# Four of eight weight-chunk turns moved from TensorE to DMA transposes on ScalarE's queue

## The chip, the cores and the metric

The kernel runs on one core of a Trainium2 chip. The metric is device time in microseconds (us) for one launch, the median over runs. The engines are named as in the profile: PE is TensorE's matmul stream and PEld its weight loads, DVE is VectorE, ACT is ScalarE, POOL is GpSimd, and SP is SyncE, which issues most DMAs. ACT can issue DMAs too, from its own instruction stream.

## The reference

Linear attention is followed by a multiplicative feed-forward network, all of it without a softmax or an activation function:

```python
kv  = einsum('bhsd,bhse->bhde', k, v)                 # 8 batches, 8 heads, 576 tokens, 64 wide
out = einsum('bhsd,bhde->bhse', q, kv)
rms = sqrt(mean(out * out, axis=-1, keepdims=True) + 1e-06)
x   = out / rms * g_norm                              # then (4608 tokens, 512)
a, b = x @ w1, x @ w2                                 # 512 -> 1024
h   = a * b @ w3                                      # 1024 -> 1024
y   = h @ w_out                                       # 1024 -> 512
```

Everything is float32 inside the kernel. The four weight arrays reach the kernel as 64-bit words and are converted there.

## The kernel before

**The fold.** Since nothing stands between w3 and w_out, the kernel first multiplies the two into one matrix w3o (1024 x 512), held in `w3o_sb`. This takes place at the start, in two halves of 512 rows each. Each half goes over eight chunks of 128 columns of w3 (`c` = 0 to 7). For a chunk, a 128x512 piece of w3 has to be turned, four blocks of 128x128, before it can be the stationary operand of four matmuls (`fold_chunk`, L694) whose sums stay in four PSUM banks over all chunks.

**The turn.** `turn_w3(half, c)` does it on PE: four transposes (L681) into a PSUM bank with the tag "at", then an ACT copy (L686) of 128x512 into a place in the tile `ab`. There are four such places, one for each `c % 4`, and three "at" banks, which the turns share with query turns (L355), kv sums (L335), and products of attention (L413). The turn of chunk c+1 stands ahead of the last matmul of chunk c.

**What else is in the fold's second half.** The order on every engine is the order in which this loop is written; nothing rearranges it. Around the second half's chunks stand parts of attention for batch 0:
- `begin_q` (ahead of c = 1 and c = 4): eight PE transposes of queries in two "at" banks and two ACT copies `qT` (L357). `begin_kv`: 72 small matmuls (L335) into two "at" banks and six small ACT copies of the sums.
- `product` (behind c = 2 and c = 5): 64 small matmuls (L413), then the norm in steps: two squares on ACT (L380), two reduces on DVE (L381), the root on ACT (L385), the reciprocal (L387) and two multiplies (L390) on DVE, which write `xn`.
- `x_first`: the result of the first product is turned by DMA: `turn_by_dma` copies the 32-bit words apart into two planes of 16-bit words (a split, L294 or L296), issues a 16-bit DMA transpose on SP (L298), and puts the planes together again (a merge, L308).
- the conversion of the remaining raw weights in units of 128x1024 words. A unit has two ACT passes (L158, L160; `begin_next`) and four DVE operations (L162, L166, L169, L172; `end_next`); a unit of w1 and w2 is also scaled by `g_norm` on DVE (L135). The second half's units are numbered here by their place in the list `todo`: 8, 9, 11 and 13 hold the w3 chunks 0 and 1, 2 and 3, 4 and 5, 6 and 7 of the second half, and 10 and 12 are w1 and w2 units. One unit is ended, and the next begun, around each chunk.
- loads on SP: raw weights (L198), queries (L94), k and v (L104).

After the fold the kernel computes the feed-forward network by groups of 512 tokens, with fewer products by sums and differences of blocks (`winograd`, L724, L1016, L1274), and prepares the next batches of attention beside it. The w1 and w2 matmuls of the first group (L724) begin at 83.21 us.

The loop of the second half, as it was:

Of the kernel before, what the change touches and what calls it, by code (L numbers as in the profile page):

```python
# [22 lines left out]
def kernel(  # L23
# [32 lines left out]
    nc = tc.nc  # L56
    PSUM = bass.MemoryType.PSUM
    P = 128
# [5 lines left out]
    KF = DF // P  # L64
# [19 lines left out]
    def bank(pool, tag):  # L84
        return pool.tile([P, 512], FP32, name=tag, tag=tag)
# [6 lines left out]
    def load_q(b, r):  # L92
        t = loaded["q", b, r] = inp.tile([P, 2, J * D], FP32, name="q_sb")
        nc.sync.dma_start(  # L94
            out=t, in_=q[b, 2 * r:2 * r + 2, 0:G, :].rearrange("h (p j) d -> p h (j d)", j=J)
        )
# [20 lines left out]
    ab = [ab_all[:, i] for i in range(2)]  # L117
# [73 lines left out]
    def load_next():  # L191
        if len(raws) == len(todo):
            return
        what, i = todo[len(raws)]
        raw = raw_tile()

        def load(where, src):
            nc.sync.dma_start(out=raw[:, where].rearrange("p (c m) -> p c m", c=src.shape[1]), in_=src)  # L198

        if what == "w":  # L200
            for n, w in enumerate((w1, w2)):
                src = w[:, i * P:(i + 1) * P].rearrange("(c p) f -> p c f", p=P)
                load(slice(n * 512, (n + 1) * 512), src)
        elif what == "b":
            for h in range(2):
                src = w3[DF // 2:DF, (2 * i + h) * P:(2 * i + h + 1) * P]
                load(slice(h * 512, (h + 1) * 512), src.rearrange("(m p) f -> p m f", p=P))
        else:
            src = w3[0:DF // 2, i * P:(i + 1) * P].rearrange("(m p) f -> p m f", p=P)
            cols = w_out[i * P:(i + 1) * P, :].rearrange("p (c f) -> p c f", c=1)  # L210

            n = 1 if i else 2
            for h in range(n):
                load(slice(h * 512 // n, (h + 1) * 512 // n), src[:, h * NH // n:(h + 1) * NH // n, :])
            for h in range(n):
                f = slice(h * DM // n, (h + 1) * DM // n)
                load(slice(512 + f.start, 512 + f.stop), cols[:, :, f])
        raws.append(raw)

    converted = []  # L220
# [14 lines left out]
    begun = []  # L235
    in_first_group = False

    def begin_next(between=None):
        if len(begun) < len(todo):
            begun.append(conversions(len(begun)))  # L240
            for c in begun[-1]:
                next(c)
                if between is not None:
                    between()
                next(c)

    def end_next(load=True):
        for c in begun[len(converted)]:
            all_of(c)
        converted.append(len(converted))  # L250
        if load:
            load_next()

    def all_of(steps):
        for _ in steps:
            pass
# [14 lines left out]
    def keep_warm(n):  # L271

        t = bank(ps_mm, "mm")
        for _ in range(n):
            nc.tensor.matmul(t[:, 0:P], lhsT=ident, rhs=ident, start=True, stop=True)

    def turn_by_dma(srcs, apart, turned, dsts, copy=nc.gpsimd.tensor_copy):

        def words(t):
            return t.bitcast(U16).rearrange("p ... (n w) -> p ... n w", w=2)

        def planes(t, i, n):
            t = t.bitcast(U16).rearrange("p (w n) -> p w n", w=2)
            size = 4 * P // n
            return t[:, :, i * size:(i + 1) * size]

        for i, src in enumerate(srcs):  # L290
            to = planes(apart, i, len(srcs))
            if len(src.shape) == 3:
                src, to = words(src), to.rearrange("p w (a n) -> p w a n", a=src.shape[1])
                copy(to, src.rearrange("p a n w -> p w a n"))  # L294
            else:
                copy(to, words(src).rearrange("p n w -> p w n"))  # L296
        yield
        nc.sync.dma_start_transpose(  # L298
            out=turned.bitcast(U16).rearrange("p (a t) -> p a t", t=P), in_=apart.bitcast(U16)
        )  # L300
        yield
        for i, dst in enumerate(dsts):
            src = planes(turned, i, len(dsts))
            if len(dst.shape) == 3:
                src = src.rearrange("p w (a n) -> p a n w", a=dst.shape[1])
            else:
                src = src.rearrange("p w n -> p n w")
            copy(words(dst), src)  # L308
# [365 lines left out]

    w3T = {}

    def turn_w3(half, c):
        t_ps = bank(ps_at, "at").rearrange("p (m f) -> p m f", m=NH)
        for m in range(NH):
            src = chunks[:, c, 0, m * P:(m + 1) * P]  # L680
            nc.tensor.transpose(t_ps[:, m, :], src, ident)  # L681

        w3T[half, c] = ab[c % 4 // 2][:, c % 2].rearrange(
            "p i (a f) -> p (i a) f", f=P
        )
        nc.scalar.copy(w3T[half, c], t_ps)  # L686

    sums_ps = {}

# [700 lines left out]
    chunks = fold.tile([P, KF, 2, DM], FP32, name="chunks")  # L1390
    with tc.manual_schedule(
        engines={mybir.EngineType.DVE, mybir.EngineType.Activation, mybir.EngineType.SP}
    ):
        for _ in range(RAW):
            load_next()
        nc.scalar.activation(const.tile([P, 1], FP32, name="warm"), eps_col, AF.Sqrt)
        g_row = const.tile([1, P], FP32, name="g_row")
        for e in range(2):
            nc.scalar.dma_start(
                out=g_row[:, e * D:(e + 1) * D], in_=g_norm.rearrange("(o d) -> o d", o=1)  # L1400
            )


        keep_warm(14)
        begin_next()
        end_next()
        turn_w3(0, 0)
        keep_warm(9)
        begin_next()

        g_ps = bank(ps_at, "at")[:, 0:1]
        nc.tensor.transpose(g_ps, g_row, ident[0:1, 0:1])
        nc.scalar.copy(g_col, g_ps)
        for c in range(KF):

            if c:
                begin_next()
            end_next()
            if c == 4:
                load_four("k", 0, 0)  # L1420
                load_q(0, 0)
            elif c == 5:
                load_four("v", 0, 0)
                load_q(0, 1)
                load_q_left(0)
            fold_chunk(0, c, range(NH - 1))
            if c == 0:
                begin_next(lambda: turn_w3(0, 1))
            else:
                turn_w3(*((0, c + 1) if c + 1 < KF else (1, 0)))  # L1430
            fold_chunk(0, c, [NH - 1])
            if c == 0:
                keep_warm(2)


        first = batch(0)
        first.start()
        BEGIN, PRODUCT = {1: 0, 4: 1}, {2: 0, 5: 1}
        norms = {}
        FIRST = len(converted) + KF - 1  # L1440
        for c in range(KF):
            if c in BEGIN:
                first.begin_q(2 * BEGIN[c], 2 * BEGIN[c] + 1)
                if c == max(BEGIN):
                    x_first = first.x_by_dma(0, nc.scalar.copy)
                    next(x_first)
                    next(x_first)
            if c - 1 in norms:
                all_of(norms[c - 1])
            if c < KF - 2:  # L1450
                if c < max(BEGIN):
                    begin_next()
                if c == max(BEGIN) + 1:
                    all_of(x_first)

                end_next(len(raws) < FIRST)
            elif c == KF - 2:
                run(sum_w(0))
            fold_chunk(1, c, [0])
            if c in BEGIN:  # L1460
                first.begin_kv(BEGIN[c])
                if c == max(BEGIN):
                    load_q_left(1)
            if c + 1 == KF:
                for r in range(2):
                    first.turn(2 + r)
                run(combine_x(0))
                end_next(False)
                for _ in range(3):
                    load_next()  # L1470
            fold_chunk(1, c, range(1, NH - 1))
            if c + 1 < KF:
                turn_w3(1, c + 1)
            if c in (max(BEGIN), KF - 2):
                begin_next()
            fold_chunk(1, c, [NH - 1])
            if c in PRODUCT:
                norms[c] = first.product(PRODUCT[c])
                next(norms[c])
                next(norms[c])  # L1480
    fold_cm.__exit__(None, None, None)
    late_pool = ctx.enter_context(tc.tile_pool(name="late", bufs=1, reuse_waits="tile"))
# [6 lines left out]
    for n, T in enumerate(groups):  # L1489
# [29 lines left out]
        if T in IN_TWO:  # L1519
            p = 2  # L1520
# [130 lines left out]
```

## Time and profile before

| | |
|---|---|
| median of 3 runs | 744.86 us (744.6 to 745.33) |
| the profiled execution's own time | 745.0 us |
| its span, first to last instruction | 743.1 us |
| PE busy | 736.6 us (99%) |
| DVE, ACT busy | 629.4 us (85%), 378.7 us (51%) |
| granted TensorE clock | 1.000 |
| fold's second half and the attention in it, on PE | 46.66 to 83.21 us from its second turn on |

The profiled execution's time is 1.9 us longer than its span. A line of the chain of waits gives a start, a length and the work that the end of the program rests on at that time; a line of a timeline gives a start, the time from the first to the last of a run of equal instructions, and in brackets how long the engine had been idle and whom it waited for. L12 is line 12 of the kernel.

### The profile page before, as it was taken

The page shows a single profiled execution, that of the slowest core. Times are in us where ns is not written, and L with a number is a line of the kernel's source. Part 1 is how long each engine was busy: PE and PEld are TensorE (multiplying, and loading weights), DVE is VectorE, ACT ScalarE, POOL GpSimd, SP SyncE. Part 2 cuts the span into 40 slices and gives each one's busy share as a digit, 9 for nine tenths or more (in the row PEclk, how much of TensorE's full clock was granted, in tenths as well). Part 3 has the DMA queues.
Part 4 walks back from the last instruction along what each step waited for, and adds up shares of the span by engine and source line. Part 5 has one row for each costly group of instructions (what it writes and reads, how often), then busy time and mean ns, then how long its engine had stood idle before and what let it go on. Part 6 is the DMA issues. An engine that isn't in the chain of part 4 may idle for free.

```text
span 743.1 us, 16816 instructions
## 1 busy us (share of the span) xinstructions
PE 736.6 (99%) x6843; PEld 659.5 (89%) x6843; DVE 629.4 (85%) x1233; ACT 378.7 (51%) x652; POOL 21.8 (3%) x29
## 2 busy tenths in 40 slices
PE   8999999999999999999999999999999999999998
PEld 6455788888899999999999999999999999999997
DVE  6987998967869689978996899689969987997797
ACT  6687778424552575257526752576277313212321
POOL 0000000132000000010000001000001000000000
PEclk9999999999999999999999999999999999999999
DMA  9996934599999698869886988588848662565454
GB/s 307 366 321 208 263 108 122 122 331 307 281 307 321 176 264 271 267 159 284 258 265 158 304 255 263 184 279 241 278 101 220 220 212 87 176 215 162 135 198 135
DMA packets 135456, 169.65 MB, mean 228 GB/s; under 512 B 78036, under 2 KB 110804, under 8 KB 135380
## 3 DMA queue, kind: packets, MB, share of 16 engines
q1 hardware_dynamic: 132928, 154.16, 69.6%
q10 hardware_dynamic: 2452, 14.42, 5.7%
q8 instruction: 54, 0.88, 0.5%
q14 instruction: 22, 0.18, 0.1%
HBM read 130.55 MB, written 20.71 MB: 204 GB/s over the span
## 4 chain that ended last, share of the span: by engine, by line
PE 96%; DVE 1%; ACT 1%; DMA 1%; issue 0%; SPq 0%; ACTq 0%
PE mm L724 37%; PE mm L1274 23%; PE mm L1016 21%; PE mm L694 7%; PE at L335 2%; PE at L724 2%; PE at L413 1%; PE mm L413 1%; PE at L681 1%; DMA raw<-in_moe_w_out_dram 1%; PE at L1317 0%; DVE ab L162 0%; PE at L432 0%; ACT w_sb L133 0%; DVE chunks L169 0%
## 5 line engine op out<-in xcount | busy, mean ns | idle before, releaser
L1065 ACT COPY slots<-mm 128x512 f32<-128x512 f32 x88 | 51.7, 587 | 125.7 <-PE mm L1274 83.1
L724 PE MATMUL mm<-xT,w_sb 128*128 128x256 f32 x448 | 102.9, 379 | 0.0
L724 PEld LDWEIGHTS mm<-xT,w_sb 128*128 128x128 f32 x448 | 84.4, 190 | 11.5 <-issue 0.5
L724 PE MATMUL mm<-xc,ws 128*128 128x256 f32 x336 | 76.1, 379 | 0.0
L724 PEld LDWEIGHTS mm<-xc,ws 128*128 128x128 f32 x336 | 63.8, 190 | 8.7
L742 ACT COPY slots<-mm 128x512 f32<-128x512 f32 x59 | 34.6, 587 | 70.9 <-PE mm L724 65.5
L694 PE MATMUL mm<-chunks,ab 128*128 128x512 f32 x128 | 60.7, 605 | 0.7 <-DVE chunks L172 0.7
L1069 DVE TENSOR_TENSOR slots<-mm,slots 128x512 f32<-128x512 f32 x66 | 45.1, 683 | 17.3 <-PE mm L1016 17.3
L1066 ACT COPY slots<-mm 128x384 f32<-128x384 f32 x88 | 42.4, 482 | 25.8 <-PE mm L1274 23.1
L1016 PE MATMUL mm<-ws,w3o_sb 128*128 128x128 f32 x350 | 53.9, 275 | 0.0
L381 DVE TENSOR_REDUCE inv<-sq 128x8 f32<-128x512 f32 (+1 forms) x40 | 24.6, 629 | 29.9 <-ACT sq L380 29.9
L1274 PE MATMUL mm<-w3o_sb,ab 128*128 128x128 f32 x368 | 49.0, 276 | 0.0
L1016 PEld LDWEIGHTS mm<-ws,w3o_sb 128*128 128x128 f32 x350 | 46.4, 192 | 0.0
L1274 PEld LDWEIGHTS mm<-w3o_sb,ab 128*128 128x128 f32 x368 | 45.4, 192 | 0.6
L1274 PE MATMUL mm<-w3o_sb,raw 128*128 128x128 f32 x340 | 43.5, 275 | 0.0
L694 PEld LDWEIGHTS mm<-chunks,ab 128*128 128x128 f32 x128 | 21.6, 190 | 22.4 <-issue 14.4
L1274 PEld LDWEIGHTS mm<-w3o_sb,raw 128*128 128x128 f32 x340 | 40.7, 192 | 0.0
L724 PE MATMUL mm<-xc,w_sb 128*128 128x256 f32 x160 | 38.6, 384 | 0.3 <-ACT slots L742 0.3
L724 PE MATMUL mm<-xT,ws 128*128 128x256 f32 x160 | 38.1, 381 | 0.0
L1070 DVE TENSOR_TENSOR slots<-mm,slots 128x384 f32<-128x384 f32 x66 | 36.4, 551 | 1.9 <-PE mm L1274 1.9
L308 ACT COPY xT<-xn 128x1024 uint16<-128x1024 uint16 x28 | 32.5, 1168 | 3.3 <-DMA xn<-xT 3.3
L724 PEld LDWEIGHTS mm<-xc,w_sb 128*128 128x128 f32 x160 | 29.7, 190 | 4.9 <-ACT slots L742 0.7
(243 smaller groups left out, 1650.8 us busy)
## 6 DMA issues: line engine op xcount, KB each, us to landing
w3o_sb<-w_l SPq DMA_DIRECT2D x21, 896.0 KB, 4.9
w3o_sb<-w3o_l SPq DMA_DIRECT2D x18, 896.0 KB, 6.8
raw<-in_moe_w_dram SPq DMA_DIRECT2D x31, 512.0 KB, 7.4
raw<-w3o_l SPq DMA_DIRECT2D x15, 896.0 KB, 4.9
w3o_sb<-w3o_l ACTq DMA_DIRECT2D x14, 896.0 KB, 4.6
k_sb<-in_k_dram SPq DMA_DIRECT2D x16, 576.0 KB, 5.1
v_sb<-in_v_dram SPq DMA_DIRECT2D x16, 576.0 KB, 6.3
q_sb<-in_q_dram SPq DMA_DIRECT2D x32, 256.0 KB, 4.3
```

The source lines that it names most:

```text
L308: copy(words(dst), src)
L335: nc.tensor.matmul(ps[r * D:(r + 1) * D, :], lhsT=k_sb[rows, r, cols], rhs=v_sb[rows, r, cols], start=(j == 0), stop=(j == JS - 1),)
L381: adds["norm"] = nc.vector.tensor_reduce(out=inv[:, i], in_=sq.rearrange("p (h d) -> p h d", d=D), axis=AX.X, op=ALU.add)
L694: nc.tensor.matmul(sums_ps[half][m], lhsT=w3T[half, c][:, m, :], rhs=chunks[:, c, 1, :], start=(c == 0), stop=(c == KF - 1),)
L724: nc.tensor.matmul(ps[:, u, :], lhsT=lhsT(a_name, u, c), rhs=rhs(b_name, c),  start=(u == 0 and c == 0 and new), stop=(c == chunks - 1), s ...
L742: copies.setdefault(name, []).append(nc.scalar.copy(t, ps))
L1016: nc.tensor.matmul(ps[place // 4][:, place % 4, :], lhsT=x, rhs=y, start=new and place // 4 not in seen, stop=True, skip_group_check=True,)
L1065: nc.scalar.copy(z[:, 0:4], ps[0])
L1066: return nc.scalar.copy(z[:, 4:7], ps[1][:, 0:3])
L1069: nc.vector.tensor_add(z[:, 0:4], ps[0], z[:, 0:4])
L1070: nc.vector.tensor_add(z[:, 4:7], ps[1][:, 0:3], z[:, 4:7])
L1274: nc.tensor.matmul(ps[place // 4][:, place % 4, :], lhsT=x[:, c, :], rhs=y[:, c, :], start=new and place // 4 not in seen, stop=(c == 1), ...
```

## The change

In the fold's second half the chunks 2, 3, 4 and 5 are no longer turned on PE. VectorE splits the natural 128x512 piece into two planes of 16-bit words in its place in `ab`, a DMA transpose issued on ScalarE's queue turns the planes and writes them over the natural piece, and an ACT copy merges them into the place in `ab`. The chunks 0, 1, 6 and 7, and the whole first half, stay on PE.

The places of the steps in the loop are: splits and issues for 2 and 3 at c = 0, behind the end of unit 9; their merges at c = 1, behind the end of unit 10; splits of 4 and 5 at c = 2, behind the end of unit 11, and their issues behind the middle matmuls of c = 2; the merge of 4 between the squares and the root of the first norm; the merge of 5 at c = 3, where the turn for chunk 4 was. At c = 2 the four DVE operations of unit 12 are also issued, ahead of the first norm's; the scale by `g_norm` stays where it was, behind that norm.

```diff
-    def turn_by_dma(srcs, apart, turned, dsts, copy=nc.gpsimd.tensor_copy):
+    def turn_by_dma(
+        srcs, apart, turned, dsts, copy=nc.gpsimd.tensor_copy, split=None, queue=nc.sync
+    ):
...
-                copy(to, words(src).rearrange("p n w -> p w n"))
+                (split or copy)(to, words(src).rearrange("p n w -> p w n"))
         yield
-        nc.sync.dma_start_transpose(
+        queue.dma_start_transpose(
             out=turned.bitcast(U16).rearrange("p (a t) -> p a t", t=P), in_=apart.bitcast(U16)
         )
...
+    def w3_by_dma(c):
+        natural, to = chunks[:, c, 0, :], place_w3(1, c).rearrange("p m f -> p (m f)")
+        return turn_by_dma(
+            [natural], to, natural, [to], nc.scalar.copy, split=nc.vector.tensor_copy,
+            queue=nc.scalar,
         )
...
                 end_next(len(raws) < FIRST)
+                if c == 0:
+                    split_w3(2, 3)
+                    send_w3(2, 3)
+                elif c == 1:
+                    all_of(turns[2])
+                    all_of(turns[3])
+                elif c == 2:
+                    split_w3(4, 5)
+                    for steps_of_w in begun[len(converted)]:
+                        next(steps_of_w)
...
             fold_chunk(1, c, range(1, NH - 1))
-            if c + 1 < KF:
+            if c == 2:
+                send_w3(4, 5)
+            elif c == 3:
+                all_of(turns[5])
+            if c + 1 < KF and c + 1 not in turns:
                 turn_w3(1, c + 1)
...
                 norms[c] = first.product(PRODUCT[c])
                 next(norms[c])
+                if c == 2:
+                    all_of(turns[4])
                 next(norms[c])
```

`split_w3` runs the first step of `w3_by_dma` for each of its chunks, `send_w3` the second, and `all_of` the rest.

More of the change, by code (lines that the diff above doesn't have):

```diff
@@ L293, in turn_by_dma @@
                 src, to = words(src), to.rearrange("p w (a n) -> p w a n", a=src.shape[1])
-                copy(to, src.rearrange("p a n w -> p w a n"))
+                (split or copy)(to, src.rearrange("p a n w -> p w a n"))
             else:
-                copy(to, words(src).rearrange("p n w -> p w n"))
+                (split or copy)(to, words(src).rearrange("p n w -> p w n"))
         yield
-        nc.sync.dma_start_transpose(
+        queue.dma_start_transpose(
             out=turned.bitcast(U16).rearrange("p (a t) -> p a t", t=P), in_=apart.bitcast(U16)
@@ L675, with place_w3 @@
     w3T = {}
+    def place_w3(half, c):
+        w3T[half, c] = ab[c % 4 // 2][:, c % 2].rearrange("p i (a f) -> p (i a) f", f=P)
+        return w3T[half, c]
     def turn_w3(half, c):
@@ L681, in turn_w3 @@
             nc.tensor.transpose(t_ps[:, m, :], src, ident)
-        w3T[half, c] = ab[c % 4 // 2][:, c % 2].rearrange(
-            "p i (a f) -> p (i a) f", f=P
+        nc.scalar.copy(place_w3(half, c), t_ps)
+    def w3_by_dma(c):
[3 more added lines that the diff above has]
+            queue=nc.scalar,
         )
-        nc.scalar.copy(w3T[half, c], t_ps)
     sums_ps = {}
@@ L1440, with split_w3, send_w3 @@
         FIRST = len(converted) + KF - 1
+        turns = {}
+        def split_w3(*cs):
+            for c in cs:
+                turns[c] = w3_by_dma(c)
+                next(turns[c])
+        def send_w3(*cs):
+            for c in cs:
+                next(turns[c])
         for c in range(KF):
```

## The prediction

> **What bounds the kernel now.** I read the page first (shares by engine, then the chain that ended last), then the chain of waits between 44 and 84 us, then the timelines of ScalarE and VectorE there, then the DMA share by window and the DMA transposes' own rows.
>
> ```profile
> PE 736.6 (99%) x6843; PEld 659.5 (89%) x6843; DVE 629.4 (85%) x1233; ACT 378.7 (51%) x652; POOL 21.8 (3%) x29
> ...
> PE 96%; DVE 1%; ACT 1%; DMA 1%; issue 0%; SPq 0%; ACTq 0%
> ```
>
> TensorE (PE) is never idle for long: what leaves PE's stream may leave the time, if nothing else then comes last. ACT's 51% is an average over the whole span, so I look at the stage itself. The chain between 44 and 84 us is all PE:
>
> ```profile
> 46.66 0.44 PE at L681 x4
> 47.09 0.86 PE mm L694 x2
> 47.95 0.87 PE at L355 x8
> 48.83 0.86 PE mm L694 x2
> ...
> 52.81 0.44 PE at L681 x4
> ...
> 56.82 0.44 PE at L681 x4
> ...
> 58.12 1.09 PE at L413 x64
> ...
> 61.98 0.44 PE at L681 x4
> ...
> 63.28 0.87 PE at L355 x8
> ...
> 65.28 1.21 PE at L335 x72
> ...
> 68.40 0.44 PE at L681 x4
> ```
>
> Columns: start, length, what. The L681 pieces are the chunk turns; those at 52.81, 56.82, 61.98 and 68.40 (chunks 2 to 5) go. The second query turn (63.28) and the second kv product (65.28) stay. ScalarE beside them:
>
> ```profile
> 57.35 0.59 ACT L686 COPY ab<-at 128x512 f32<-128x512 f32 x1 [1.33 <-PE at L681]
> 59.26 1.09 ACT L380 ACTIVATE sq<-at 128x512 f32<-128x512 f32 x2 [1.32 <-PE at L413]
> 61.20 0.31 ACT L385 ACTIVATE inv<-inv,eps_col 128x16 f32<-128x16 f32 x1 [0.86 <-DVE inv L381]
> 61.42 1.17 ACT L158 ACTIVATE ab<-raw 128x1024 f32<-128x1024 uint32 x1
> 62.47 1.16 ACT L160 ACTIVATE chunks<-raw 128x1024 f32<-128x1024 f32 x1
> 63.51 0.60 ACT L686 COPY ab<-at 128x512 f32<-128x512 f32 x1
> 63.97 1.09 ACT L357 COPY qT<-at 128x512 f32<-128x512 f32 x2
> ```
>
> ACT waits for PE (brackets) up to the norm, and from the square root at 61.20 on it runs without a gap until 66.96. The first query copy ends at 63.97 + 0.60 = 64.57, only 0.71 before kv starts on PE at 65.28, and kv's second bank waits for that copy.
>
> **PE.** Removed: 16 transposes, 4 x 0.44 = 1.76 us. Nothing is added to PE. 1.76 is 0.24% of 744.86; about 0.2% (1.49 us) is what a measurement of this kernel can tell from no change, so nearly all of it must survive to count as faster.
>
> **Splits on VectorE.** Four copies of 128x1024 16-bit words. No row shows one on DVE. Bounds: 0.69 (TENSOR_SCALAR 128x1024, one source) and 1.23 (two-source 128x1024, L162); ScalarE's own split of that shape (L294) took 1.08. I take 0.69, since the form is one-source, SBUF to SBUF, and keep 1.23 for the range. The first two follow unit 9's last operation (ends 44.73) and delay unit 10 from 45.62 to 46.1; the 0.38 us that DVE idled before unit 11 (50.60) takes most of that up, so unit 11 ends at about 54.7 instead of 54.53. Splits 4 and 5 then end at 56.1, inside the 5.36 us in which DVE waits for the squares (L381 at 59.89).
>
> The Trainium skill's page "VectorE: DVE Perf Modes" (the perf-mode tier table) gives a one-source 16-bit copy in SBUF four times the base rate, 693 ns for 2048 elements, half of that here plus the fixed part; no run here shows one. By it, an estimate, each split would be some 0.3 us shorter than by the row, and the time a few tenths of a us lower at most.
>
> **DMA transposes on ScalarE's queue.** The 66 transposes of the trace (all on SP) took 1.23 to 3.62 us to issue, median 1.3. ScalarE's plain DMAs (0.36 us) were issued while the copy ahead of them still ran (225.80, under a copy of 225.63 to 226.11). I take 1.27 each, starting under the running L160; the other bound is 1.27 each behind it, 1.1 us later. T2 and T3 (the transposes of chunks 2 and 3) then hold ACT until 48.0, and the copy of chunk 1 ends at 48.6 instead of 47.78; c1's first weights load at 48.56: a stall of at most 0.1 (1.2 by the other bound).
>
> **Merges on ScalarE.** L308's copies of this shape took 1.17. Four merges replace four L686 copies of 0.59: +0.58 each. Merges 2 and 3 stand between unit 11's L160 and the kv copies: about 51.85 to 54.2. Kv copies end at 55.5, and unit 12's two ACT passes run 55.5 to 57.7 instead of 53.82 to 56.02: up to 1.7 later.
>
> **Unit 12 ahead of the norm.** Four DVE operations, 1.23 + 0.69 + 0.69 + 1.23 = 3.84. They can't start before unit 12's L158 ends (about 56.3 to 56.65) and end at 60.1 to 60.5. PE reaches product(0) 0.88 earlier (two turns), so the squares could be there at 58.5; the reduces start at 60.1 to 60.5, not 59.89. The 0.88 is lost here, and the norm comes 0.2 to 0.6 late. What moves behind the norm is less work for DVE, off the path.
>
> **The second norm step, and kv.** T4 and T5 are issued under unit 12's L160, from about 56.6, and ACT is free at 59.1 for the squares (59.1 to 60.2). Merge 4 follows (60.2 to 61.4, if T4 has landed), the root at 61.8 or, at the lower end, 61.4. Then unit 13 (until 64.25), merge 5 in the place of a copy (until 65.35), and the first query copy ends at 65.85 (65.4 at the lower end), against 64.57. PE, now 3 x 0.44 = 1.32 early, stands at kv at about 64.0 and waits: kv starts at 65.5 to 65.9, against 65.28. So +0.2 to +0.6 at kv, whatever PE had won or lost before. Behind it chunk 5's turn is gone (-0.44): **-0.2 to +0.2** net. ACT's copy for chunk 6 (73.61 to 74.19; chunk 6 begins on PE at 74.75) must not be late: ACT runs 1.3 behind at the splits of x (L294), 0.6 of it comes back where chunk 5's copy is gone, the rest at its waits; it ends at about 74.7, needed at about 74.9. After that PE is dense and hands the difference on unchanged.
>
> **When T4 lands.** It must land by 60.6, 4.0 us after its issue; later, each us is a us. The windows around it are full of input loads, and transposes in a full stretch looked so:
>
> ```profile
> 56.00:58.00 2.00, 2.00 (x8) 0.77 (x6) 0.00 (x0) 0.60 (x2) 0.00 (x0) 1.00 1.04 402
> 58.00:60.00 2.00, 2.00 (x67) 1.51 (x67) 0.11 (x1) 0.74 (x2) 0.00 (x0) 1.00 1.06 377
> ```
> ```profile
> L298 SPq DMA_TRANSPOSE xn<-xT x2: 3069/3346/3624, 209.2 to 212.9; - x2
> ...
> DMA to landing us min/median/max: 5.1/6.5/7.9
> ```
>
> The last two columns of the windows are DMA share and GB/s: full. The second fence is line L298 between 208 and 213 us (DMA share 1.10 around it). In quiet stretches a transpose landed after 2.8; in 184 to 190 us (share 1.16) three landed after 4.6, 3.0 and 2.8. I take 4.5, between these: +0.5. Likeliest sum: +0.1 + 0.5 = +0.6. The profiled run took 745.0, 0.14 above the median, so I add to the median: 744.86 + 0.6 = 745.5.
>
> The Trainium skill's page "VectorE: DVE Perf Modes" (the rules for kernel authors) says to turn 128x128 on TensorE where a PSUM destination is fine and by DMA otherwise, with 390 against 1309 ns a block. Against the rows: PE pays 0.44 for four blocks here, a DMA transpose 1.27 of a sequencer and 2.8 or more until it lands. By that rule alone the change loses; by the rows it is the cover that decides.
>
> **Rivals.** (1) Forecast, 0.50: what PE wins is given back at kv because ACT comes last; -0.2 to +1.4, that is 744.7 to 746.3.
>
> (2) All hidden, 0.15: -1.76, 743.1. For it: PE has 1.76 us less to do and idles nowhere now. Against: ACT's row of operations from the root at 61.2 to the first query copy is 0.3 + 1.05 + 1.05 + 1.15 + 0.6 = 4.15, so kv can't begin before 65.4 unless the root comes over 1 us earlier; that needs DVE's unit 12 to end before 59.
>
> (3) Slower, 0.35: a DMA transpose holds ScalarE at merge 4, between the squares and the root (59 to 64 us), and with it norm, query copies and kv. It decides from a landing of 5.4 us on (+0.1 + 1.4 = the bound of 1.49). At 6.5, the mean of the fence, +2.6: 747.5. For it: share 1.04 to 1.06. Against: the loads there end by 60.2. A second way to this side is VectorE: with splits at 1.23, unit 12 ends 4 x 0.54 = 2.2 later, less some 0.6 that DVE waits for ACT anyway: +1.6, 746.6. Issue behind L160 instead of under it adds 1.1 to either.
>
> (4) That the transposes don't start early, since the queue is ScalarE's and not free, is in (3). That the PE work is not really gone can't be: the order of PE's instructions shows 16 fewer.
>
> **Numbers.** Likeliest 745.5. Range 743.2 (nearly all of rival 2) to 747.9 (rival 3 with a landing of 6.5 and some of the other bounds; 7.9 is left out). Faster by over 0.2% 0.15, within 0.50, slower 0.35.
>
> **What would show it.** L681 16 transposes fewer, 1.76 us. DVE's splits: 0.69 or more. L381 of the first norm at 60.1 to 60.5, PE waiting about 1.3 us at kv (L335) for L357's copy, and ACT without a gap from the root to there. If L381 starts before 59.5 or kv before 64.8, rival 2 holds; if ACT idles before merge 4 for a DMA, rival 3. The prediction is wrong if PE shows no wait between 60 and 75 us, or if the time moves elsewhere than before 75 us.

## The result, and the profile after

The changed kernel takes 751.01 us (median of 6 runs, 749.74 to 752.89), the kernel before 744.96 (6 runs, 744.6 to 745.33): a ratio of 1.0083, 95% interval 1.0066 to 1.0099. It is slower by 6 us, outside the range that was predicted. Its profiled run took 751.92, with a span of 750.0 against 743.1.

The page, shares by engine and the chain that ended last:

```profile
PE 737.3 (98%) x6827; PEld 659.0 (88%) x6827; DVE 633.2 (84%) x1237; ACT 380.0 (51%) x652; POOL 21.6 (3%) x29
...
PE 89%; DMA 4%; ACT 4%; DVE 1%; issue 1%; ACTq 0%; SPq 0%; DVEq 0%
```

PE has its 16 transposes fewer (6827 against 6843 instructions) and yet is not less busy. Of the chain, 7% have left PE (96% before); DMA and ScalarE have 4% each, against 1% before. Where, the chain of waits between 40 and 95 us says (start, length, what):

```profile
47.52 2.96 ACTq L300
...
50.52 0.09 ACT ab L689
...
57.84 7.08 DMA chunks<-ab
64.95 0.78 ACT ab L310
...
88.08 7.12 PE mm L734 x33
```

ACTq L300 is ScalarE's sequencer issuing a DMA transpose; "DMA chunks<-ab" is the transpose of chunk 4 (T4) from issue to landing. The first group's matmuls begin at 88.08 instead of 83.21. ScalarE's own row shows both (start, length, in brackets the idle time before and its releaser):

```profile
46.08 4.40 ACTq L300 DMA_TRANSPOSE chunks<-ab  x2
50.52 0.59 ACT L689 COPY ab<-at 128x512 f32<-128x512 f32 x1 [3.41 <-DVE w_sb L172]
...
59.21 3.19 ACTq L300 DMA_TRANSPOSE chunks<-ab  x1
62.44 1.09 ACT L382 ACTIVATE sq<-at 128x512 f32<-128x512 f32 x2 [2.77 <-issue]
64.95 1.16 ACT L310 COPY ab<-chunks 128x1024 uint16<-128x1024 uint16 x1 [1.42 <-DMA chunks<-ab]
```

The copy of chunk 1 runs at 50.52, not 47.19, since the issue of the second transpose (T3) takes 2.96 us and the copy is queued behind it. (The releaser named in its bracket, DVE's L172, is only what came last by semaphore events; the copy doesn't need that tile.) The squares wait the same way for the issue of T5, 3.19 us. Then the merge of chunk 4 waits for T4, and root, norm, query copies and kv stand behind the merge. On PE:

```profile
51.16 1.13 PE L704 MATMUL mm<-chunks,ab 128*128 128x512 f32 x2 [1.87 <-ACT ab L689]
...
67.50 1.09 PE L357 MATMUL at<-ident,q_sb 128*128 128x128 f32 x4 [2.64 <-ACT ab L158]
68.37 1.92 PE L704 MATMUL mm<-chunks,ab 128*128 128x512 f32 x2
```

PE loses 1.87 us ahead of chunk 1 and 2.64 at the second half of the query turns, whose bank waits for the norm's output (the first multiply of L392 ends at 67.40 and PE goes on at 67.50; L158 in the bracket is again only what else ended then). Behind the second wait PE also runs slower: these four transposes take 1.09 instead of 0.60, the two matmuls of 68.37 take 1.92 instead of 1.12. The windows say why (the third number from the end is the granted clock, then DMA share and GB/s):

```profile
66.00:68.00 2.00, 0.51 (x3) 0.54 (x4) 1.55 (x4) 2.00 (x4) 0.00 (x0) 0.78 0.43 126
68.00:70.00 2.00, 2.00 (x5) 0.71 (x3) 2.00 (x3) 2.00 (x4) 0.00 (x0) 0.50 0.10 24
70.00:72.00 2.00, 2.00 (x74) 1.55 (x74) 1.93 (x3) 2.00 (x3) 0.00 (x0) 0.87 0.35 115
```

The sum to 88.08: the start of the second half was already 0.46 late in this run (turn of chunk 0 at 43.08 against 42.62, in code that is the same); waits 1.87 + 2.64 + 0.20 = 4.71; the slower pieces behind the second wait 0.49 + 0.80 + 0.12 (kv) = 1.4; less 1.76. Together 4.8 of the 4.87. This is an account of PE's row, and the 1.4 us of slower pieces did not by themselves set 88.08. From the root on, which comes at 66.01 instead of 61.20, the chain runs over ScalarE and the DMA transposes of x to the copy for chunk 6, and nothing in that stretch waits for PE:

```profile
70.38 1.89 ACT xT L296 x2
...
73.73 2.82 DMA xn<-xT
...
76.65 2.24 ACT xT L310 x2
...
78.91 0.60 ACT ab L689
79.51 0.04 issue
79.55 2.84 PE mm L704 x6
```

At full clock PE would have stood some 1.6 us ahead of chunk 6 instead of 0.20. That is worked out from these rows; no run tried it.

Some 2 us more come later in this run: from 194 to 258 us, around a wait of DMA, the distance to the kernel before grows by 1.36, and at 497 by 0.8.

### The profile page after: what moved, and what is told of

Read it like the earlier page. It is cut to its first block, busy times and chain, and to the rows that moved or that the text cites. A ratio compares the mean times of both kernels' runs of the same rounds, so it can differ in the third digit from the quotient of the medians.

```text
span 750.0 us, 16792 instructions
## 1 busy us (share of the span) xinstructions
PE 737.3 (98%) x6827; PEld 659.0 (88%) x6827; DVE 633.2 (84%) x1237; ACT 380.0 (51%) x652; POOL 21.6 (3%) x29
## 4 chain that ended last, share of the span: by engine, by line
PE 89%; DMA 4%; ACT 4%; DVE 1%; issue 1%; ACTq 0%; SPq 0%; DVEq 0%
PE mm L734 36%; PE mm L1284 21%; PE mm L1026 21%; PE mm L704 4%; PE at L337 2%; PE at L734 2%; DMA xn<-xT 1%; DMA raw<-in_moe_w_out_dram 1%; PE mm L415 1%; DMA chunks<-ab 1%; PE at L415 1%; DMA w3o_sb<-w3o_l 1%; ACT ab L158 1%; DMA raw<-in_moe_w_dram 1%; PE at L687 0%
```

## Experiments

Two theories were set against each other. **A**: the loss is the DMA path, namely the transposes' issue on ScalarE (A1) and their late landing behind loads (A2). **B**: the loss is engine time, merges, splits and the moved unit.

**The DMA transposes left out.** Splits, merges and the moved unit stay; chunks 2 to 5 stay unturned.

```diff
-        queue.dma_start_transpose(...)
+        if queue is nc.sync:
+            queue.dma_start_transpose(...)
...
+            if queue is not nc.sync:
+                src = words(turned)
             copy(words(dst), src)
```

> The changed kernel without its four DMA transposes: splits and merges run in their shapes and places, the weight unit stays moved, and chunks 2 to 5 are left unturned. Theory A (the DMA path is the whole loss): what is left is the prediction's ledger of engine time, -0.2 to +0.2 against before, 744.8 to 745.3 at a before of 745.0; kv on PE starts at about 65.5 after a wait of about 1.3 for ScalarE's query copy. Theory B (merges, splits and the moved unit are the loss): 748 or more.

745.18 against 745.05, ratio 1.0000 (0.9991 to 1.0010). Theory B falls: with all the engine work of the change in place, the time is that of before, as the prediction's ledger had it. ScalarE without the transposes:

```profile
58.34 1.08 ACT L385 ACTIVATE sq<-at 128x512 f32<-128x512 f32 x2 [1.35 <-PE at L418]
59.31 1.05 ACT L313 COPY ab<-chunks 128x1024 uint16<-128x1024 uint16 x1
61.01 0.31 ACT L390 ACTIVATE inv<-inv,eps_col 128x16 f32<-128x16 f32 x1 [0.65 <-DVE inv L386]
```

The merge (1.05 here, 1.16 where the words lie in planes) fits between squares and root, and the root comes at 61.01 (before: 61.20). What PE won it lost again in small waits for ScalarE: 0.14 at the query turn, 0.63 at kv, 0.50 ahead of chunk 6. So the whole +6 is the DMA path, and the +0 beneath it is ScalarE, which has no room for what PE gave up.

**The moved unit alone**, no DMA turns.

```diff
                 end_next(len(raws) < FIRST)
+                if c == 2:
+                    for steps_of_w in begun[len(converted)]:
+                        next(steps_of_w)
```

> The kernel before with one part of the change alone: the four DVE operations of unit 12 ahead of the first norm, no DMA turns. In the row of before they can run from 55.0 (end of unit 12's first ACT pass) to 58.9, and the reduces start at 59.89: no change, 744.7 to 745.4. If VectorE's order matters by itself: the reduces start after 59.9 and the time is 0.5 to 1 longer.

745.17 against 745.25, ratio 0.9999 (0.9990 to 1.0008): it costs nothing by itself.

**The queue.** `queue=nc.sync` in place of `queue=nc.scalar`.

> The four DMA transposes issued by SyncE, all else as changed. Theory A1 (mainly the issue holds ScalarE): the copy of chunk 1 is ready at about 48.3 and not at 51.1, the first stall of PE (1.87) is gone, the squares of the first norm run at 59 instead of 62.4; the merge of chunk 4 still waits for its transpose; 746 to 747.5. Theory A2 (mainly the late landing behind the loads that were queued before): the first stall goes, but the second one at the query turn (2.64) stays or grows, since on SyncE's queue the transposes stand behind k, v and raw loads too, and loads stand behind them: 748 to 750. Theory B (engine time): no change from 751.

752.65 against 745.09, 1.0099 (1.0074 to 1.0124). ScalarE is no longer held by an issue, and the first stall is gone; the second is larger than all of them were:

```profile
47.00 0.59 ACT L689 COPY ab<-at 128x512 f32<-128x512 f32 x1 [0.53 <-PE at L687]
...
58.35 1.09 ACT L382 ACTIVATE sq<-at 128x512 f32<-128x512 f32 x2
65.57 1.16 ACT L310 COPY ab<-chunks 128x1024 uint16<-128x1024 uint16 x1 [6.14 <-DMA chunks<-ab]
```

T4 was issued at 55.87, when k, v and a unit of raw weights had been queued from 53.67 to 55.78, and landed 9.60 later; PE waited 6.05. The direction is A2, and its upper end, 750, was passed, and the granted clock stood at 0.50 to 0.51 from 68 to 74 afterwards.

**One pair at a time**, on ScalarE's queue as in the change: only chunks 2 and 3, or only 4 and 5.

> Only chunks 2 and 3 by DMA transposes on ScalarE's queue, 4 and 5 turned on PE as before; the weight unit stays moved. Theory A: the stall before chunk 1 (1.87) is there, 2 x 0.44 of PE's turns are saved, the norm runs without a merge between squares and root; PE is 1.0 late after chunk 1 and nothing gives more: about +1.0 to +1.5, 746.0 to 746.5. Theory B (the loss goes with the number of merges and splits): half of +6, about 748.

> Only chunks 4 and 5 by DMA transposes on ScalarE's queue, 2 and 3 turned on PE as before; the weight unit stays moved. Theory A: no stall before chunk 1, but the second transpose's issue (about 3) holds the squares and the merge of chunk 4 waits for a landing of about 7 us: the root at about 64.5 to 65.5 instead of 61.2, kv late by 3 to 4, less 0.44 for chunk 5's turn: +2.5 to +4, 747.5 to 749. If x3 and x4 add to about the whole (+6), the two pairs are independent. Theory B: half of +6, about 748, without a wait for a DMA in ScalarE's row.

Chunks 2 and 3: 748.30 against 745.09, 1.0047 (1.0033 to 1.0062), 2 us above what theory A gave. By the number alone theory B (about 748) would have it, but the kernel without transposes has ruled B out, and the rows show where the time goes. The stall ahead of chunk 1 is 2.25, and there are two more that I had not counted, 0.47 and 0.18 around the query turns: merges and kv copies run late, so unit 12's ScalarE passes run from 57.67 and its four DVE operations, now ahead of the norm, hold the reduces (the root waits 1.92 us for them). The moved unit is free only while ScalarE is on time. Chunks 4 and 5: 750.08, 1.0061 (1.0044 to 1.0078), 1 us above theory A's upper end. T4 landed 8.92 after its issue, T5's issue took 3.99; PE waited 2.35 (for the copy of chunk 3, which stood behind that issue), 0.43 and 0.61. The two excesses, 3.2 and 5.0, add to more than 6: the pairs aren't independent. T4's landing of 8.9 here against 7.1 with both pairs fits a second pair that is issued later, when fewer loads are left ahead; that was not tried by itself.

**Loads behind the transposes**, on SyncE's queue.

```diff
-                end_next(len(raws) < FIRST)
+                end_next(c > 2 and len(raws) < FIRST)
                 if c == 0:
                     split_w3(2, 3)
                     send_w3(2, 3)
+                    load_next()
...
             if c == 2:
                 send_w3(4, 5)
+                load_next()
+                load_next()
```

> The four transposes on SyncE's queue, and three loads of raw weights put behind them: the load of c = 0 behind those of chunks 2 and 3, the loads of c = 1 and c = 2 behind those of chunks 4 and 5. Theory A2 (a transpose starts only when all that was queued before it on either queue is through): the transposes of 4 and 5 start at about 58 instead of 61.7 and land by 61, the wait of ScalarE for the merge of chunk 4 (6.14 in the run with SyncE's queue alone) falls under 1, and the time is the ledger's: 744.8 to 745.8. Rival A3 (a transpose is slow beside any load, in whatever order): the wait stays at 4 to 6, 749 to 752.

746.70 against 745.05, 1.0025 (1.0015 to 1.0035).

```profile
55.49 4.04 SPq L300 DMA_TRANSPOSE chunks<-ab  x2
59.59 2.22 SPq L198 DMA_DIRECT2D raw<-in_moe_w_dram  x4
```
```profile
60.84 1.16 ACT L310 COPY ab<-chunks 128x1024 uint16<-128x1024 uint16 x1 [1.29 <-DMA chunks<-ab]
```

The order of queueing decides, not the queue and not the transposes as such: with 3 units of raw weights moved behind them, and nothing else changed against the kernel with SyncE's queue alone (752.65), 6 us are back. The merge of 4 still waits 1.29, for k and v are ahead of it, and PE waits 0.91, 0.72 and 1.23; that is 1 us more than expected.

**Loads later, transposes on ScalarE's queue.**

```diff
-                end_next(len(raws) < FIRST)
+                end_next(c > 2 and len(raws) < FIRST)
...
                 first.begin_q(2 * BEGIN[c], 2 * BEGIN[c] + 1)
+                for _ in range(1 if c == 1 else 2):
+                    load_next()
```

> The changed kernel as it is, its transposes on ScalarE's queue, with three raw loads moved later on SyncE's: the load of c = 0 behind the first query turns (issued about 49), those of c = 1 and c = 2 behind the unit of c = 3 and the second query turns (62 and later). Theory A2 (order of queueing over both queues): the first transpose's data starts at 47.4 instead of 49.3 and the second issue ends about 2 earlier, so the stall before chunk 1 falls from 1.9 to under 0.6; only k and v are ahead of the second pair, the root comes at 62 instead of 66; 745.0 to 746.5. Rival A4 (ScalarE's own queue is slow for transposes whatever else is queued): the second issues still take 3, the stalls stay, 749 or more.

757.41 against 745.25, 1.0169 (1.0156 to 1.0183). The time lies on A4's side (749 or more), but the rows do not bear A4 out: the first pair went as A2 had it, the rest did not. ScalarE and SyncE:

```profile
45.58 2.71 ACTq L300 DMA_TRANSPOSE chunks<-ab  x2
48.34 0.59 ACT L689 COPY ab<-at 128x512 f32<-128x512 f32 x1 [1.73 <-PE mm L704]
```
```profile
67.59 3.13 SPq L198 DMA_DIRECT2D raw<-in_moe_w_dram  x4
71.27 6.34 SPq L300 DMA_TRANSPOSE xn<-xT  x2
```

With one unit of raw loads less ahead of them T2 and T3 were issued in 1.33 + 1.27, and PE's wait ahead of chunk 1 fell from 1.87 to 0.18: ScalarE's queue is not slow in itself. For the second pair the edit missed its aim: SyncE ran ahead of the program's place and issued a raw load at 52.48 all the same, so T5's issue took 3.64 and PE waited 3.79. The loads that did move now stood ahead of the transposes of x on SyncE, whose two issues took 6.34 together instead of 2.70; PE waited 4.02 for what follows from them. A transpose behind loads is slow at a third place.

**Only two chunks**, 2 and 3, on SyncE's queue, the load of c = 0 behind them, the unit in its old place.

> Only chunks 2 and 3 by DMA transposes, on SyncE's queue, with the load of c = 0 behind them, and the weight unit where it was before the change. PE has 8 transposes fewer, 0.88 us; ScalarE's two merges (1.16 each) fall where it used to wait for PE (0.52, 1.33, 1.32 in the row of before), so the norm can come 0.88 earlier. Theory A2 with full cover: -0.88, 744.1. If ScalarE's time is not covered even for two chunks: 745.0 to 745.5.

744.88 against 745.05, 0.9998 (0.9989 to 1.0007): no difference that can be told. In the fold the gain is there: PE has no wait, and from its second turn to the first group's matmuls 82.35 - 46.85 = 35.50 us pass, against 83.21 - 46.66 = 36.55 before.

```profile
46.85 0.44 PE at L687 x4
...
82.35 3.67 PE mm L734 x17
```

In the profiled run 0.86 of lead at 82 us were 0.66 at 190 us and 0.10 at the end; most of it went at 490 us, where PE stood 0.42 us within the small matmuls of a product without a releaser in the profile. Several of these runs show a wait there, from 0.15 to 0.94. What it is was not found.

**Three chunks**, 2, 3 and 5, with the merge of 5 behind the query copies.

> Chunks 2, 3 and 5 by DMA transposes on SyncE's queue, two raw loads behind them, the weight unit in its old place, the merge of 5 behind the query copies; chunk 4 stays on PE, so that no merge stands between the squares and the root. PE has 12 transposes fewer, 1.32 us. If ScalarE's row still covers it, the first group's matmuls start 1.3 earlier than before from the second turn on, and the time is 743.8 to 744.5; as in the kernel with two chunks some of it may be lost again later. If the merge of 5 makes the copy of chunk 6 late, 744.5 to 745.0.

745.30 against 745.25, 1.0006 (0.9997 to 1.0015). ScalarE's copy for chunk 6 comes last, PE waits 1.06 for it, and 83.16 - 47.05 = 36.11 us pass: more moved off PE, less gained than with two.

**GpSimd for the splits and merges of x**: `first.x_by_dma(0)` in place of `first.x_by_dma(0, nc.scalar.copy)`, once with all four chunks and the loads behind them, once with three.

> As the kernel with the loads behind the transposes, and the splits and merges of the first product's x (4.2 us of ScalarE between the query copies and the copy of chunk 6) on GpSimd. If ScalarE's row behind kv is what ends last there, the copy of chunk 6 comes about 3 earlier and nothing is lost after kv: up to -0.44 against the kernel with the loads behind, 744.4 to 745.3; the wait at kv itself (1.3 for ScalarE's query copy) stays.

> As the kernel with three chunks (2, 3 and 5) and, besides, the splits and merges of the first product's x on GpSimd instead of ScalarE (4.2 us of ScalarE's row between the query copies and the copy of chunk 6). In the kernel with three chunks PE waited 1.06 us for that copy, and 36.1 us passed from its second turn to the first group's matmuls, against 36.55 before. If ScalarE's row was the only thing in the way, the wait is gone and 35.2 us pass (-1.32); the time is 743.9 to 744.6. If GpSimd's copies or the transposes behind them come last instead, PE waits at another place and the time stays at 745.0 to 745.5.

With four, 745.76 against 745.05, 1.0013 (1.0005 to 1.0022), 0.9 below the kernel with the loads behind and 0.5 above what was expected: the wait ahead of chunk 6 is gone, those at query turn and kv stay (0.61, 0.74). With three, 748.64 against 744.93, 1.0051 (1.0032 to 1.0069), above both ranges, with a new wait, on VectorE:

```profile
62.47 3.41 POOL L296 COPY xT<-xn 128x1024 uint16<-128x1024 uint16 x2 [61.17 <-DVE xn L392]
```
```profile
63.45 1.53 DVE L166 TENSOR_SCALAR w_sb<-w_sb 128x1024 f32<-128x1024 f32 x1
65.02 1.41 DVE L169 TENSOR_SCALAR w_sb<-w_sb 128x1024 uint32<-128x1024 uint32 x1
66.46 1.22 DVE L172 CUSTOM_DVE_ANT_0 w_sb<-w_sb,ab 128x2048 uint16<-128x2048 uint16 x1
```

While GpSimd copies (62.47 to 65.88), VectorE's L166 and L169 take 1.5 and 1.4 instead of 0.69. The conversion of chunks 6 and 7 comes late, and PE waits 1.29 for it and 1.69 later. No version was found that is faster than the kernel before by more than the measurement can tell.

## Why the prediction was wrong

- **The landing of T4** was the term that failed most. I put 4.5 between rows of 2.8 to 7.9 and left 7.9 out. It measured 7.1 in the changed kernel, 8.9 and 9.6 in two others. The rows were averaged as if the landing were a property of a busy stretch. It is what is queued ahead: in the changed kernel's trace the first packet of T2 is at 49.04, 3.0 after its issue, and the first of T4 at 61.88, 4.0 after, both when the raw loads issued before them on SyncE's queue are nearly through (the last two, issued at 55.47 and 55.91, landed at 62.5 and 64.4). The profile of before showed a DMA share above 1.0 up to 60 (and of 1.10 from 43 to 48, ahead of T2), and the price could have been read there: behind those loads T4, issued at 56.6, would have started at about 60 (an estimate). The order is not strict: with 4 and 5 alone, T4's packets began at 59.59, 4.0 after its issue, and ran beside the last loads until about 62.
- **The issue** was the second. I took 1.27 for each transpose, with 1.1 as the further cost of the other bound. The first of each pair took 1.33 and 1.25, the second 2.96 and 3.19, while SP's rows up to 3.62 were on the table. The stall ahead of chunk 1, "at most 0.1 (1.2 by the other bound)", measured 1.87; the squares, expected at 59.1, ran at 62.44.
- **The rules cited.** The Trainium skill's page "DMA: Bandwidth & Descriptors" (Issuing engines are not separate DMA queues) says that DMAs of scalar, sync and gpsimd run on the same 16 engines and interleave, whoever started them. The first half agrees with these traces: ScalarE's queue gave T2 and T4 no way around SyncE's loads. That they interleave shows only late: T2's packets begin at 49.04, 3.0 after its issue, T4's 4.0 after. The Trainium skill's page "VectorE: DVE Perf Modes" would by the prediction's reading have made a split 0.3 shorter than the row. But it gives the fourfold rate only where the elements of every tensor lie at step 1 (What auto-detection actually checks), and a split reads every second word; the splits measured 0.69, as the row had it.
- **Engine time** was right. Splits 0.69, merges 1.16, PE 16 transposes less, "-0.2 to +0.2 net" against a ratio of 1.0000 once the transposes are left out, and the moved unit at nothing, 0.9999. The total was right by some luck: without the transposes PE waited 0.14, 0.63 and 0.50 at three places, the last of them ahead of chunk 6, where the prediction had nothing, and not 1.3 at kv.
- **Rival 3 was the mechanism**, a transpose that holds ScalarE between squares and root. Its price was too small. It had the landing alone, at 6.5: +2.6. By its own rule (+0.1, and a us for each us over 4.0) a landing of 7.1 gives +3.2, and the later issue (57.84, not 56.6) and the held squares come on top.
- **The wait's place**: I had PE standing 1.3 us at kv for the query copy. With the norm this late, it stands before, at the query turns' second bank (2.64).
- **Open** is the part behind the fold: the profiled run loses 2 us more after 190 us, the runs spread over 3.2 us against 0.7 before, and no experiment here isolates that. The prediction had named time that moves elsewhere than before 75 us as a sign of being wrong, and this part did.

## What to carry to other kernels

Before a DMA goes onto a path that something waits for, add up what is queued ahead of it at its time of issue on every queue that shares the engines: in these traces its landing was about that backlog plus its own time, and another engine's queue was no way around. A queue on a compute engine costs more than the first issue: here a second transpose held ScalarE until just after the first had begun to move (packets from 49.04 and 61.88, the second issues over at 50.48 and 62.40), and all that is written behind it waited too. Work taken off a bound engine is won only where the next engine has slack at that place, and here two chunks filled it.

## What was not expected of the hardware

- The granted TensorE clock fell to half with long waits of PE. After 2.64 us of waiting it was 0.50 in the 2 us window behind, with 0.78 and 0.87 in the windows beside it; after 2.35 us likewise (0.77, 0.50, 0.87); after 6.05 us it stayed at 0.50 for three windows, where kv took 2.20 instead of 1.28. After 1.87 and 2.25 us it stayed at 1.00. It is not the length of the wait alone. The traces' clock records have low stretches of 3.41 us (67.11 to 70.53 in the changed kernel, 63.09 to 66.51 with 4 and 5 alone) or of 6.83, and within the kernel every change comes a whole number of 3.41 us after the one before it. Cut into such stretches, PE stood for 2.03 to 3.41 us of each one that ended in a fall, and for at most 1.69 us of any at full clock that did not; the wait of 2.25 us fell into two of them, 1.55 and 0.70. The Trainium skill's page "TensorE: Matmul & The Clock Gate" (Part 1) puts the fall to half at one idle window or more, some 3.4 us; the length of the stretches agrees, but here 2.03 us of standing within one were enough.
- GpSimd's copies of 128x1024 16-bit words doubled VectorE's one-source operations beside them (0.69 to 1.5 and 1.4), and in each of the two kernels a two-source one (L162: 2.06 and 2.17 instead of 1.22); another L162 that ran beside such a copy took 1.22.
